# Attention and gated layer on one core: the inner layer's columns dealt in pairs

## The chip, the cores and the metric

The kernel runs on one core of one Trainium2 chip. The metric is the device time of one execution in microseconds. Three runs of the kernel before gave a median of 287.04 us (286.77 to 288.16).

## The reference

Inputs are float32: q, k and v of 8 batches, 8 heads, 576 positions and 64 channels; `w_in` (512 x 2048), `w_out` (2048 x 512) and `beta` (2048).

```python
q_s = softmax(q, over the channels);  k_s = softmax(k, over the positions)
kv  = einsum('bhsd,bhse->bhde', k_s, v)
att = einsum('bhsd,bhde->bhse', q_s, kv)
x   = att.transpose(0, 2, 1, 3).reshape(4608, 512)
h   = x @ w_in
g   = h * (1 / (1 + exp(-beta * h)))
out = g @ w_out
```

The 2048 columns of `w_in` are the rows of `w_out` and the entries of `beta`: the inner layer. Any order of them gives the same sum, so long as all three use the same.

## The kernel before

The five engines take their instructions from one list of named steps, `ORDER` at the top of the file, written out by hand; each engine takes its own steps in that order, and SP issues nearly all the loads and stores. A layer under the kernel adds the semaphore waits: where an instruction touches what an instruction of another engine wrote or still reads, it waits for that one.

*Attention.* Per batch b, `ld q`, `ld k`, `ld v` bring in the inputs; DVE takes maxima (`qmax`, `kmax`), POOL subtracts them (`qsub`, `ksub`), ACT takes exponentials (`qexp`, `kexp`), DVE sums and inverts (`qsum`, `qrcp`), POOL normalises (`qnorm`). PE multiplies k by v (`kv`, line 638), transposes q (`qtr`, line 464; later batches by DMA) and forms x transposed (`x`, line 688), which ACT and DVE cast into `xT` (`xev`).

*Inner layer.* The 4608 rows of x make 9 chunks of 512. A chunk has 16 units u of 128 inner columns. Step `h n` (n = 16 x chunk + u, function `st1`, line 889) is four matmuls, one for each contraction tile kt of 128: the weights are a 128 x 128 block of `w_in_b`, the moving side 512 columns of `xT`, the result a bank of PSUM. `th n` (ACT, line 907) takes the tanh with the scale in `beta_c[:, u]`, `g n` (DVE, line 924) makes the gated value, and `o n` (`st2`, line 959) multiplies it by `w_out_b[:, u, :]` into four accumulators. In the first chunk the first four units are cut into halves of 256 columns (`h 0 0 0`: unit 0, half 0, contraction tiles 0 and 2; `h 0 0 1`: tiles 1 and 3), and the order is h 0, 1, 2, 3, 6, 4, 5, 7, then 8, 10, 9, 11 with the transposes of batch 1 between.

*Weights.* They come in eight blocks `w0` to `w7`, in turn `w_in` and `w_out`: w0, w2, w4, w6 are 512 columns each of `w_in`, w1, w3, w5, w7 are 512 rows each of `w_out`. A block comes in two halves (`ld w2 0`, `ld w2 1`), each 512 KB, into one of four float32 stages `wst`; a half of a `w_in` block is two of the four contraction tiles. `cast w2 0` and so on turn a half into bfloat16, on POOL or ACT as `ORDER` says. Block w0 is cast in two parts, so that unit 0 is ready early: columns 0 to 127 (`cast w0 0 0`, `cast w0 1 0`) and 128 to 511 (`cast w0 0 1` on POOL, `cast w0 1 1` on ACT). `w_in_b` holds 2048 columns for each contraction tile, in their own order.

*Beta.* One DMA brings `beta` as 16 rows of 128; PE transposes it (line 345) and ACT copies it into `beta_c`, one column for each unit.

Step names of POOL around the change, in its order: `cast w0 0 1`, `qsub 1 0`, `qnorm 0 2`, `cast w2 0`, `cast w2 1`, `qsub 1 1`, `cast w1 0`, `cast w1 1`, `cast w4 0`, `qnorm 1 0`, `qnorm 1 1`, `cast w3 0`, `cast w6 0`.

Of the kernel before, what the change touches and what calls it, by code (L numbers as in the profile page):

```python
# [8 lines left out]
BF16 = mybir.dt.bfloat16  # L9
F32 = mybir.dt.float32  # L10
ALU = mybir.AluOpType
ACTF = mybir.ActivationFunctionType
# [105 lines left out]
def kernel(  # L118
# [11 lines left out]
    P = 128  # L130
    B, H, S, D = q.shape
    DM, FF = w_in.shape
# [4 lines left out]
    KT = DM // P  # L137
    NJ = FF // P
# [13 lines left out]
    def op(name, fn, eng=None):  # L152
        assert name not in ops, name
        ops[name] = (fn, eng)
# [4 lines left out]
    def sbt(name, shape, dt):  # L159
        return sb.tile(shape, dt, name=name)  # L160

    ident_f = sbt("ident_f", [P, P], F32)
# [2 lines left out]
    minus = sbt("minus", [P, P], F32)  # L165
    warm = sbt("warm", [P, P], BF16)
    first = sbt("first", [P, 1], F32)
    beta_rows = sbt("beta_rows", [NJ, P], F32)
    beta_c = sbt("beta_c", [P, NJ], F32)
    w_in_b = sbt("w_in_b", [P, KT, FF], BF16)  # L170
    w_out_b = sbt("w_out_b", [P, NJ, DM], BF16)
    wst = [sbt(f"wst{i}", [P, 4, 512], F32) for i in range(4)]
    qf = [sbt(f"qf{i}", [P, KT, NI, D], F32) for i in range(2)]
# [21 lines left out]
    th = [sbt(f"th{i}", [P, 512], BF16) for i in range(3)]  # L195
# [5 lines left out]
    place = {}  # L201
# [4 lines left out]
    def take(*who):  # L206
        assert sum(last in done for last, _ in turns) >= len(who), who
        for w in who:
            n = next(n for n, (last, _) in enumerate(turns) if last in done)
            i = turns.pop(n)[1]  # L210
            place[w] = ring[i][:]
            turns.append((w, i))

    def made(what, *parts):
        done.update((what, p) for p in parts)

    def uses(what, *parts):
        for p in parts:
            assert (what, p) in done, (what, p)
# [7 lines left out]
    dve, act, pool, pe, sp = nc.vector, nc.scalar, nc.gpsimd, nc.tensor, nc.sync  # L227
    ENGINES = {"act": act, "dve": dve, "pool": pool}

    def cast(eng, dst, src):  # L230
        if eng is act:
            act.copy(dst, src)  # L232
        else:
            eng.tensor_copy(dst, src)  # L234
# [57 lines left out]
    for b in range(B):  # L292
        n = 2 if b else 1
# [4 lines left out]

    W = [(w, blk) for blk in range(4) for w in ("i", "o")]
    w_in_v = w_in.rearrange("(kt p) f -> p kt f", p=P)
    w_out_v = w_out.rearrange("(j p) f -> p j f", p=P)

    def load_w(n, half):
        which, blk = W[n]
        if n > 3:
            which, blk = W[n - 4]
            if which == "i":
                uses("i", *[(4 * blk + u, half) for u in range(4)])  # L310
            else:
                uses("o", 2 * blk + half)
            which, blk = W[n]
        dst = wst[n % 4][:, 2 * half : 2 * half + 2, :]
        if which == "i":
            sp.dma_start(dst, w_in_v[:, 2 * half : 2 * half + 2, 512 * blk : 512 * blk + 512])
        else:
            sp.dma_start(dst, w_out_v[:, 4 * blk + 2 * half : 4 * blk + 2 * half + 2, :])

    def cast_w(n, half, eng, c0=0, c1=512):  # L320
        which, blk = W[n]
        s = wst[n % 4][:, 2 * half : 2 * half + 2, c0:c1]
        if which == "i":
            made("i", *[(4 * blk + c // P, half) for c in range(c0, c1, P)])
            cast(eng, w_in_b[:, 2 * half : 2 * half + 2, 512 * blk + c0 : 512 * blk + c1], s)
        else:
            made("o", 2 * blk + half)
            cast(eng, w_out_b[:, 4 * blk + 2 * half : 4 * blk + 2 * half + 2, :], s)

    for n in range(8):  # L330
        for half in range(2):
            op(f"ld w{n} {half}", lambda n=n, half=half: load_w(n, half))
            if n == 0:
                for c, (c0, c1) in enumerate(((0, P), (P, 512))):
                    op(
                        f"cast w{n} {half} {c}",
                        lambda e, n=n, half=half, c0=c0, c1=c1: cast_w(n, half, e, c0, c1),
                        "pool",
                    )
            else:  # L340
                op(f"cast w{n} {half}", lambda e, n=n, half=half: cast_w(n, half, e), "pool")

    def beta_tr():
        take("beta")
        pe.transpose(place["beta"][:, 0:NJ], beta_rows[:], ident_f[0:NJ, 0:NJ])

    def beta_ev():
        done.add("beta")
        act.copy(beta_c[:], place["beta"][:, 0:NJ])

    op("ld beta", lambda: sp.dma_start(beta_rows[:], beta.rearrange("(j p) -> j p", p=P)))
    op("beta tr", beta_tr)
    op("beta ev", beta_ev)

# [427 lines left out]
    for h in range(3):  # L782
        i0, i1 = 4 * h, min(4 * h + 4, NI)
        for J in range(2):
            p = dict(j=2 * J, n=2, i0=i0, i1=i1)
# [57 lines left out]
    def chunk_x(c):  # L843
        if c == TAILS:
            return xTt
        return xT[(c if c < TAILS else c - 1) % 2]

    def halves(h):
        return (0, 1) if h is None else (h,)

    def cols(h):
        return slice(0, 512) if h is None else slice(256 * h, 256 * h + 256)
# [3 lines left out]
    def bank(n, h):  # L856
        key = ("h", n) if h is None else ("hp", n // 2, h)
        if key not in place:
            take(key)
        if h is None:  # L860
            return place[key]
        return place[key][:, 256 * (n % 2) : 256 * (n % 2) + 256]

    def turn(n, h):
        return n if h is None else 2 * (n // 2) + h

    def st1(n, ks=(0, 1, 2, 3), h=None):
        c, u = divmod(n, NJ)
        x = chunk_x(c)
        for kt in ks:  # L870
            uses("i", (u, kt // 2))
            if c == TAILS:
                uses("xTt", *[(b, kt % 2) for b in range(B)])
            else:
                uses("xT", *[(c - (c > TAILS), kt, a) for a in halves(h)])
        if h is not None and n % 2 and ks[0] == 0:
            uses("st1", (n - 1, h))
        if ks[0]:
            uses("begun", (n, h))
        made("begun", (n, h))  # L880
        w = bank(n, h)
        if c == 0 and h is None:
            w = w.rearrange("p (h c) -> p h c", h=2)
        for kt in ks:
            r = x[:, kt, cols(h)]
            if c == 0:
                r = x_first[:, kt % 2, kt // 2]
                r = r if h is None else r[:, h]
            pe.matmul(  # L889
                w,  # L890
                w_in_b[:, kt, u * P : (u + 1) * P],
                r,
                start=(kt == 0),
                stop=(kt == KT - 1),
            )
        if KT - 1 in ks:
            made("st1", *[(n, a) for a in halves(h)])

    def tanh(n, h=None):
        u = n % NJ  # L900
        mates = [n] if h is None else [2 * (n // 2), 2 * (n // 2) + 1]
        uses("st1", *[(m, a) for m in mates for a in halves(h)])
        if turn(n, h) >= 3:
            uses("gated", turn(n, h) - 3)
        made("tanh", *[(n, a) for a in halves(h)])
        c = cols(None if h is None else n % 2)
        act.activation(th[turn(n, h) % 3][:, c], bank(n, h), ACTF.Tanh, scale=beta_c[:, u : u + 1])  # L907

    def gate(n, h=None):
        mates = [n] if h is None else [n, n + 1]  # L910
# [88 lines left out]
    for n in range(NU):  # L999
        if n < LEAD:  # L1000
            for h in range(2):
                for x in range(2):
                    op(f"h {n} {h} {x}", lambda n=n, h=h, x=x: st1(n, (x, x + 2), h))
                op(f"th {n} {h}", lambda n=n, h=h: tanh(n, h))
                if n % 2 == 0:
                    op(f"g {n} {h}", lambda n=n, h=h: gate(n, h))
                op(f"o {n} {h}", lambda n=n, h=h: st2(n, h))
            continue
        if n in (16, 17):
            op(f"h {n} 0", lambda n=n: st1(n, (0, 1)))  # L1010
            op(f"h {n} 1", lambda n=n: st1(n, (2, 3)))
        else:
            op(f"h {n}", lambda n=n: st1(n))
        op(f"th {n}", lambda n=n: tanh(n))
        op(f"g {n}", lambda n=n: gate(n))
        if n >= NU - LAST:
            for t in range(3):
                op(f"o {n} {t}", lambda n=n, t=t: st2(n, ts=[t]))
            for x in range(2):
                op(f"o {n} 3 {x}", lambda n=n, x=x: st2(n, ts=[3], xs=[x]))  # L1020
        else:
            op(f"o {n}", lambda n=n: st2(n))
# [12 lines left out]
    with tc.manual_schedule():  # L1035
        for name, _, e in plan:
            fn, eng = ops[name]
            eng = e or eng
# [31 lines left out]
```

## Time and profile before

| | |
|---|---|
| median of three runs | 287.04 us |
| the profiled execution's time | 287.31 us |
| its span, first to last instruction | 285.5 us |
| PE busy in the span | 275.8 us (97%) |
| weight loads busy | 129.9 us (45%) |
| DVE, ACT, POOL busy | 194.9, 174.2, 131.2 us |
| `w_out` loads, 8 of 512 KB, from issue to landing | 11.2 us |
| `w_in` loads, 8 of 512 KB, from issue to landing | 7.9 us |

All times come from one execution. PE is TensorE's matmuls, PEld its weight loads, which overlap the matmuls; DVE is VectorE, ACT ScalarE, POOL GpSimd, SP the engine that issues DMAs. Rows of a group give line, engine, operation, output and input tiles with shapes and count, then busy time and mean duration in ns, then the idle time of the engine just before and what ended it. Rows of the timeline give start and duration in us, and rows of the chain of waits start, duration and what the chain ran through.

### The profile page before, as it was taken

Reading aid. Unit: us, or ns where it says so; the run is one execution under the profiler, and the core shown is the slowest. Engines: PE = TensorE matmul, PEld = TensorE weight load, DVE = VectorE, ACT = ScalarE, POOL = GpSimd, SP = SyncE. Lnnn points to the kernel's source line nnn. Section 1 sums busy time; section 2 is a strip of 40 time slices with the busy share of each in tenths; the row PEclk is TensorE's granted clock in tenths of the full one; section 3 lists DMA queues with packets and bytes.
Section 4 is the critical chain, followed back from the end, with each engine's and each line's share of the span. In section 5 each row is a group of like instructions: output and inputs, shape, how many; then the busy total and the mean of one; then the engine's idle time right before and its main releaser. Section 6 shows DMA issues by size and latency. Waiting matters only on the chain.

```text
span 285.5 us, 5163 instructions
## 1 busy us (share of the span) xinstructions
PE 275.8 (97%) x1947; PEld 129.9 (45%) x1977; DVE 194.9 (68%) x394; ACT 174.2 (61%) x291; POOL 131.2 (46%) x93
## 2 busy tenths in 40 slices
PE   7799999999999999999999999999999999999994
PEld 2356544444444544444444544444444444444442
DVE  2998957999899898997667858555754263435421
ACT  2498885887488577837586566564671274345422
POOL 6899996869379948083960650090020000000000
PEclk9999999999999999999999999999999999999999
DMA  7999999990991994991434927000054001005104
GB/s 229 390 391 385 384 389 391 390 336 7 276 371 43 316 275 181 295 329 41 152 119 113 189 62 193 0 3 2 0 141 164 0 0 39 0 0 187 73 0 147
DMA packets 37048, 50.01 MB, mean 175 GB/s; under 512 B 15760, under 2 KB 16160, under 8 KB 37024
## 3 DMA queue, kind: packets, MB, share of 16 engines
q1 hardware_dynamic: 36880, 49.63, 53.4%
q8 instruction: 15, 0.25, 0.3%
q10 hardware_dynamic: 144, 0.07, 0.1%
q14 instruction: 9, 0.07, 0.1%
HBM read 36.71 MB, written 9.44 MB: 162 GB/s over the span
## 4 chain that ended last, share of the span: by engine, by line
PE 91%; DMA 4%; ACT 1%; SPq 1%; issue 1%; DVE 0%
PE hT L889 43%; PE acc L959 42%; DMA kf<-in_k_dram 2%; DMA wst<-in_moe_w_in_dram 2%; PE hT L638 2%; PE hT L688 1%; SPq L275 1%; PE hT L951 1%; PE acc L951 1%; ACT w_in_b L232 0%; PE hT L464 0%; PE hT L734 0%; ACT qT L232 0%; ACT ek L612 0%; ACT ek L605 0%
## 5 line engine op out<-in xcount | busy, mean ns | idle before, releaser
L907 ACT ACTIVATE th<-hT,beta_c 128x512 bf16<-128x512 f32 (+1 forms) x148 | 96.6, 677 | 66.9 <-PE hT L889 48.5
L924 DVE SCALAR_TENSOR_TENSOR g<-th,hT 128x512 bf16<-128x512 bf16 x144 | 94.6, 680 | 58.5 <-ACT th L907 55.5
L959 PE MATMUL acc<-w_out_b,g 128*128 128x512 bf16 x543 | 130.7, 379 | 1.4 <-issue 0.8
L889 PE MATMUL hT<-xT,w_in_b 128*128 128x512 bf16 (+1 forms) x517 | 117.7, 372 | 0.7 <-issue 0.2
L889 PEld LDWEIGHTS <-w_in_b 128*128 128x128 bf16 x592 | 57.6, 98 | 64.8 <-ACT w_in_b L232 0.2
L959 PEld LDWEIGHTS <-g 128*128 128x128 bf16 x560 | 53.7, 98 | 64.5 <-issue 2.9
L560 POOL TENSOR_TENSOR kf<-kf,kmb 128x1152 f32<-128x1152 f32 (+1 forms) x15 | 38.0, 2543 | 23.6 <-DVE kmb L550 17.6
L441 POOL TENSOR_TENSOR qn<-eqe,qz 128x1152 bf16<-128x1152 bf16 (+2 forms) x20 | 34.5, 1739 | 28.0 <-DVE qz L433 18.1
L393 POOL TENSOR_TENSOR qf<-qf,qm 128x1152 f32<-128x1152 f32 (+2 forms) x20 | 34.4, 1733 | 18.4 <-issue 11.9
L378 DVE TENSOR_REDUCE qm<-qf 128x9 f32<-128x576 f32 (+2 forms) x34 | 23.3, 704 | 6.2 <-DMA qf<-in_q_dram 6.2
L422 ACT ACTIVATE eqe<-qf 128x576 bf16<-128x576 f32 (+2 forms) x34 | 21.5, 657 | 9.5 <-POOL qf L393 9.5
L232 ACT CAST xT<-hT 128x512 bf16<-128x512 f32 x19 | 12.6, 740 | 21.1 <-PE hT L688 21.1
L428 DVE TENSOR_REDUCE qs<-eqe 128x9 f32<-128x585 bf16 (+2 forms) x34 | 24.0, 713 | 0.5 <-ACT eqe L422 0.4
L490 DVE TRANSPOSE_TENSOR_REDUCE km<-kf 128x18 f32<-128x576 f32 x32 | 23.6, 754 | 0.0
L612 ACT ACTIVATE ek<-kf 128x576 bf16<-128x576 f32 x30 | 19.5, 683 | 0.9 <-DMA vf<-in_v_dram 0.9
L234 POOL CAST va<-vf 128x1152 bf16<-128x1152 f32 (+1 forms) x11 | 12.0, 1105 | 6.9 <-DMA vf<-in_v_dram 6.9
L889 PE MATMUL hT<-xTt,w_in_b 128*128 128x512 bf16 x63 | 14.9, 379 | 0.1
L234 DVE CAST xT<-hT 128x512 bf16<-128x512 f32 x9 | 6.3, 728 | 7.0 <-PE hT L688 7.0
L232 ACT COPY osb<-acc 128x512 f32<-128x512 f32 x14 | 7.8, 594 | 3.0 <-PE acc L959 3.0
L367 PE MATMUL hT<-g,warm 128*128 128x512 bf16 x21 | 7.0, 482 | 1.6 <-POOL g L240 1.5
L234 DVE COPY osb<-acc 128x512 f32<-128x512 f32 (+1 forms) x6 | 3.8, 632 | 4.9 <-PE acc L951 3.8
L638 PEld LDWEIGHTS <-ek 64*64 64x64 bf16 x576 | 5.7, 106 | 2.2 <-issue 1.3
(74 smaller groups left out, 121.7 us busy)
## 6 DMA issues: line engine op xcount, KB each, us to landing
qf<-in_q_dram SPq DMA_DIRECT2D x14, 576.0 KB, 6.9
kf<-in_k_dram SPq DMA_DIRECT2D x14, 576.0 KB, 7.7
vf<-in_v_dram SPq DMA_DIRECT2D x14, 576.0 KB, 8.4
out_dram<-osb SPq DMA_DIRECT2D x19, 256.0 KB, 2.6
wst<-in_moe_w_in_dram SPq DMA_DIRECT2D x8, 512.0 KB, 7.9
wst<-in_moe_w_out_dram SPq DMA_DIRECT2D x8, 512.0 KB, 11.2
out_dram<-wst SPq DMA_DIRECT2D x16, 256.0 KB, 3.7
qf<-in_q_dram SPq DMA_DIRECT2D x4, 288.0 KB, 4.1
```

Of the source, the lines that this page charges most:

```text
L234: eng.tensor_copy(dst, src)
L378: dve.tensor_reduce(qm[:, j : j + n, i0:i1], qf[b % 2][:, j : j + n, i0:i1], axis=AX.X, op=ALU.max,)
L393: eng.tensor_tensor(x, x, m, ALU.subtract)
L422: act.activation(eq[:, i0:i1, j : j + n, :].rearrange("p i j d -> p j i d"), x, ACTF.Exp)
L428: dve.tensor_reduce(qs[:, i0:i1, j : j + n].unsqueeze(3), x, axis=AX.X, op=ALU.add)
L441: eng.tensor_tensor(qn[b % 2][:, i0:i1, j : j + n, :], eq[:, i0:i1, j : j + n, :], z, ALU.mult)
L490: dve.tensor_reduce(km[:, j : j + n].rearrange("p j i e -> p (j i e)"), kf[b % 2][:, j : j + n].rearrange("p j i (e c) -> p (j i e) c", c=32),
L560: eng.tensor_tensor(x, x, m, ALU.subtract)
L889: pe.matmul(w, w_in_b[:, kt, u * P : (u + 1) * P], r, start=(kt == 0), stop=(kt == KT - 1),)
L907: act.activation(th[turn(n, h) % 3][:, c], bank(n, h), ACTF.Tanh, scale=beta_c[:, u : u + 1])
L924: dve.scalar_tensor_tensor(out=out, in0=of, scalar=1.0, in1=src, op0=ALU.add, op1=ALU.mult)
L959: pe.matmul(acc[t][:], g[n % NG][:, t * P : (t + 1) * P], w_out_b[:, u, :], start=(u == 0), stop=(u == NJ - 1),)
```

## The change

Inner columns are dealt in pairs of units. A pair m covers 256 columns of `w_in`; its even columns make unit 2m, its odd ones unit 2m + 1. A partition of `w_out`'s block then holds two rows that follow each other in memory, 4 KB, where it held two runs of 2 KB.

For `w_in` nothing changes on the side of the load. The cast writes a pair's 256 columns into a block of 320 (64 are never used), and a matmul's weights are read with a step of two. Casts of whole blocks write three free dimensions: two contraction tiles, two pairs, 256 columns. Block w0 is cast in parts of 256 and 256 columns. `beta` is read as 8 rows of 256, transposed in two pieces with a step of two, and the tanh finds its scale in the column of the new order.

```diff
-    beta_rows = sbt("beta_rows", [NJ, P], F32)
+    beta_rows = sbt("beta_rows", [NJ // 2, 2 * P], F32)
...
-    w_in_b = sbt("w_in_b", [P, KT, FF], BF16)
+    w_in_b = sbt("w_in_b", [P, KT, NJ // 2, 2 * P + 64], BF16)
...
-    w_out_v = w_out.rearrange("(j p) f -> p j f", p=P)
+    w_out_v = w_out.rearrange("(m p r) f -> p m r f", p=P, r=2)
...
-            sp.dma_start(dst, w_out_v[:, 4 * blk + 2 * half : 4 * blk + 2 * half + 2, :])
+            sp.dma_start(dst, w_out_v[:, 2 * blk + half])
...
-            cast(eng, w_in_b[:, 2 * half : 2 * half + 2, 512 * blk + c0 : 512 * blk + c1], s)
+            m0, m1 = 2 * blk + c0 // (2 * P), 2 * blk + c1 // (2 * P)
+            s = s.rearrange("p k (m c) -> p k m c", c=2 * P)
+            cast(eng, w_in_b[:, 2 * half : 2 * half + 2, m0:m1, 0 : 2 * P], s)
...
-                for c, (c0, c1) in enumerate(((0, P), (P, 512))):
+                for c, (c0, c1) in enumerate(((0, 2 * P), (2 * P, 512))):
...
-        pe.transpose(place["beta"][:, 0:NJ], beta_rows[:], ident_f[0:NJ, 0:NJ])
+        for r in range(2):
+            n = NJ // 2
+            pe.transpose(place["beta"][:, n * r : n * r + n], beta_rows[:, r : 2 * P : 2], ident_f[0:n, 0:n])
...
-    op("ld beta", lambda: sp.dma_start(beta_rows[:], beta.rearrange("(j p) -> j p", p=P)))
+    op("ld beta", lambda: sp.dma_start(beta_rows[:], beta.rearrange("(m q) -> m q", q=2 * P)))
...
-                w_in_b[:, kt, u * P : (u + 1) * P],
+                w_in_b[:, kt, u // 2, u % 2 : 2 * P : 2],
...
+        v = NJ // 2 * (u % 2) + u // 2
...
-        act.activation(th[turn(n, h) % 3][:, c], bank(n, h), ACTF.Tanh, scale=beta_c[:, u : u + 1])
+        act.activation(th[turn(n, h) % 3][:, c], bank(n, h), ACTF.Tanh, scale=beta_c[:, v : v + 1])
```

The list of steps is the same.

## The prediction

> **What bounds the kernel now.** I read the windows first, then the chain of waits.
>
> ```profile
> 20.30:62.00 41.70, 41.38 (x292) 20.91 (x296) 34.91 (x73) 33.86 (x58) 34.14 (x26) 1.00 1.05 388
> 62.00:281.90 219.90, 218.03 (x1510) 101.30 (x1533) 146.10 (x287) 128.93 (x211) 81.07 (x39) 1.00 0.41 120
> ...
> 20.29 0.38 PE hT L367
> 20.67 7.01 PE hT L889 x48
> 27.68 0.22 PE acc L959
> ...
> 31.24 0.86 PE hT L889 x4
> 32.11 0.45 PE hT L464 x8
> 32.55 1.73 PE hT L889 x8
> ...
> 37.32 3.46 PE hT L889 x16
> ```
>
> Columns of a window: stretch, length, then busy time of PE, weight loads, DVE, ACT and POOL, granted clock, DMA share, GB/s. From 20.3 us on PE is idle for 0.32 us up to 62 us and for 1.87 us up to 281.9 us, and the chain runs through PE almost without a break. Sixteen matmuls take 3.46 us, 216 ns each. So a PE stall after 20.3 us moves the end one for one, and a transfer or cast that comes earlier moves nothing. The DMA is full until 62 us (388 GB/s), but PE hides it.
>
> **Where the change bites: two waits in the order of work.** The casts of whole `w_in` blocks now write three free dimensions (two contraction tiles, two pairs, 256 columns) where two served before. I resolved the semaphores of both built programs to the instructions that raise them. PE's order is the same apart from one more small transpose, but these waits are new:
>
> ```
> PE   h 0 0 1, contraction tile 1 (reads w_in_b from element 2560)  waits for POOL cast w2 0
> PE   h 0 0 1, contraction tile 3 (reads from 7680)                 waits for POOL cast w2 1
> PE   h 10,    contraction tile 1 (reads from 4160)                 waits for POOL cast w6 0
> POOL cast w4 0 waits for PE h 7;  POOL cast w6 0 waits for PE h 8
> ```
>
> None carries data. Cast w2 0 starts at element 640 and ends at 640 + 2560 + 320 + 255 = 3775; h 0 0 1 reads 2560 to 2814, between the written rows. It looks as if a pattern of this many dimensions is compared by its whole span; the two-dimensional casts of before gave no such wait. Before, w2 was first waited for by h 6 and w6 by h 14. Whatever the cause, the waits stand in the program, and PE takes its instructions in order, so all the matmuls behind wait too, and ACT's tanh and DVE's gate behind them.
>
> **First stall.** POOL, in order of time:
>
> ```profile
> 18.20 0.82 POOL L234 CAST w_in_b<-wst 128x768 bf16<-128x768 f32 x1
> 18.98 2.12 POOL L393 TENSOR_TENSOR qf<-qf,qm 128x1152 f32<-128x1152 f32 x1
> 21.05 0.76 POOL L441 TENSOR_TENSOR qn<-eqe,qz 128x128 bf16<-128x128 bf16 x2
> 21.75 2.02 POOL L234 CAST w_in_b<-wst 128x1024 bf16<-128x1024 f32 x2
> 24.01 2.12 POOL L393 TENSOR_TENSOR qf<-qf,qm 128x1152 f32<-128x1152 f32 x1 [0.23 <-DVE qm L378]
> 26.07 2.02 POOL L234 CAST w_out_b<-wst 128x1024 bf16<-128x1024 f32 x2
> 28.03 1.04 POOL L234 CAST w_in_b<-wst 128x1024 bf16<-128x1024 f32 x1
> 29.66 4.31 POOL L441 TENSOR_TENSOR qn<-eqe,qz 128x1152 bf16<-128x1152 bf16 x2 [0.58 <-ACT th L907]
> 33.91 1.03 POOL L234 CAST w_out_b<-wst 128x1024 bf16<-128x1024 f32 x1
> 34.88 1.04 POOL L234 CAST w_in_b<-wst 128x1024 bf16<-128x1024 f32 x1
> ```
>
> Casts w2 0 and w2 1 are the pair at 21.75; the second ends at 23.77. POOL is busy without a gap from 18.20 to there, so they wait for POOL's turn, not for their load. The cast at 18.20 shrinks from 768 to 512 columns. By these rows:
>
> ```profile
> L234 POOL CAST w_in_b<-wst 128x1024 bf16<-128x1024 f32 x4 | 4.1, 1039 | 0.0
> L234 POOL CAST w_in_b<-wst 128x768 bf16<-128x768 f32 x1 | 0.8, 824 | 0.0
> L232 ACT CAST w_in_b<-wst 128x768 bf16<-128x768 f32 x1 | 0.8, 832 | 0.0
> L232 ACT CAST w_in_b<-wst 128x256 bf16<-128x256 f32 x2 | 0.9, 432 | 0.0
> ```
>
> 256 columns cost POOL 1039 - 824 = 215 ns, so cast w2 1 ends at 23.77 - 0.21 = 23.56. With about 0.15 us for semaphore and weight load (an estimate: POOL's start at 24.01 comes 0.09 us after the end of DVE's row at 23.18 below, and a weight load stands some 0.1 us long) the fourth matmul of the stage, which stood at 20.67 + 3 x 0.11 = 21.0, starts at 23.7. First stall: 2.7 us (2.5 to 2.95, the upper end without the shorter cast).
>
> **Second stall.** What follows on POOL hangs on PE again:
>
> ```profile
> 22.57 0.69 DVE L924 SCALAR_TENSOR_TENSOR g<-th,hT 128x512 bf16<-128x512 bf16 x1 [0.75 <-ACT th L907]
> 23.18 0.74 DVE L378 TENSOR_REDUCE qm<-qf 128x9 f32<-128x576 f32 x1
> 25.99 0.69 ACT L907 ACTIVATE th<-hT,beta_c 128x512 bf16<-128x512 f32 x1 [0.24 <-PE hT L889]
> 27.72 0.68 ACT L422 ACTIVATE eqe<-qf 128x576 bf16<-128x576 f32 x1
> 29.25 0.26 DVE L433 RECIPROCAL qz<-qs 128x18 f32<-128x18 f32 x1
> ```
>
> POOL's subtraction at 24.01 waits for the maximum at 23.18, which stands on DVE behind the first gate, which waits for tanh. The normalisation at 29.66 waits for the reciprocal at 29.25, whose exponential stands on ACT behind tanh of h 4, which waits for PE. So both move by 2.7 us with PE. From 29.66 POOL works without a gap to the end of cast w6 0 at 34.88 + 1.04 = 35.92. The matmul of h 10 that now waits for it stood at 32.55 + 0.22 = 32.77. Both are 2.7 us later, so the gap stays: 35.92 + 0.15 - 32.77 = 3.3 us. If POOL's chain moved by less than PE, the stall would shrink; the only play is POOL's 0.58 us of idleness before 29.66 and ACT's slack, so 2.7 to 3.3; I take 3.2. POOL's own two new waits don't bind: h 7 ends by 27.68 + 2.7 = 30.4, when POOL is just through the casts of `w_out` (28.1 + 2.7 = 30.8), and h 8 by 32.11 + 2.7 = 34.8 against 37.6 for cast w6 0.
>
> After it no new wait is left. POOL and the loads are then ahead of PE, so nothing else turns late; the later idle time of PE is scattered in pieces of about 0.1 us and gives back 0 to 0.3 us.
>
> **The rest of the change.** ACT's three part casts become 512 columns each: 832 + 2 x 432 = 1696 ns become 3 x 632 (halfway between the rows) = 1896, 0.2 us more. The second transpose for beta costs 0 to 0.23 us of PE. Both come ahead of 21 us and are hidden by the first stall; without it they would cost 0.1 to 0.4 us. The `w_out` loads in 4 KB runs could shorten the DMA's work, at most by what is visible as PE's idleness before 62 us, 0.32 us; I take nothing, since PE hides them. Weight loads with a step of two have no row. Their neighbours:
>
> ```profile
> L889 PEld LDWEIGHTS <-w_in_b 128*128 128x128 bf16 x592 | 57.6, 98 | 64.8 <-ACT w_in_b L232 0.2 <-issue 0.2
> L638 PEld LDWEIGHTS <-ek 64*64 64x64 bf16 x576 | 5.7, 106 | 2.2 <-issue 1.3 <-ACT ek L612 0.5 <-DVE qs L428 0.4
> L580 PEld LDWEIGHTS acc<-kf,ident_f 128*128 128x128 f32 x4 | 0.7, 188 | 1.3 <-issue 1.2
> 20.57 2.50 PEld L889 LDWEIGHTS <-w_in_b 128*128 128x128 bf16 x23 [0.18 <-issue]
> ```
>
> The lower bound is 98 ns as now, the upper one the float32 row, 188 ns, whose columns also lie four bytes apart. Both fit under the 216 ns of a 512-column matmul. Only the first 32 matmuls are half as wide (23 loads in 2.50 us, 109 ns each): at 188 ns they cost 32 x (188 - 109) = 2.5 us. I take 98, because the 0.1 us of loads is pipelined; the upper end goes into the range.
>
> **Sum.** Against the profiled execution's 287.31 us (span 285.5 and 1.8 around it): + 2.7 + 3.2 - 0.2 = 293.0 us. That execution lies 0.27 above the median of 287.04, so 292.8 for a median; I say 292.9.
>
> **Rivals.**
>
> *The clock drops in the stalls.* PE stands still for 1.7 and 0.9 us with one matmul between, and then for 3.2 us, longer than any gap in its record of before. At the start of the span matmuls run at half pace:
>
> ```profile
> 1.45 5.45 PE L367 MATMUL hT<-g,warm 128*128 128x512 bf16 x16 [1.45 <-POOL g L240]
> 4.39 0.15 PEld L367 LDWEIGHTS <-warm 128*128 128x128 bf16 x1 [0.28 <-issue]
> 4.82 0.15 PEld L367 LDWEIGHTS <-warm 128*128 128x128 bf16 x1 [0.28 <-issue]
> ```
>
> 430 ns between weight loads against 216, from 1.45 to about 5.2. If a stall brings that back for as long, it costs 3.75 / 2 = 1.9 us: 294.8 for one, 296.7 for both. The Trainium skill (TensorE: Matmul & The Clock Gate, Part 1) says that an idle window of about 3.4 us halves the clock until a busy window has passed; the second stall lies just under that, so by the rule the case is open. Against it: the stall is short of that start-up phase.
>
> *The step of two shows* as well, in the half-wide matmuls, up to 2.5 us: 295.4.
>
> *Only the first stall bites.* If POOL's normalisations and casts run early enough, h 10 waits for little: 287.1 + 2.7 = 289.8. It needs POOL's chain to come loose from PE; the two rows with waits above speak against it.
>
> *No stall.* The two casts at 21.75 are through before h 0 0 1 asks, at 20.9, and cast w6 0 before 32.8: then only part casts and the beta transpose remain, 287.2, not slower. The point is whether POOL gets to those casts 2.8 us earlier; its rows show 2.9 us of other work ahead of them, in order, which makes this unlikely.
>
> **How the numbers follow.** Forecast 0.56 (own range 292.0 to 293.7), clock 0.20, step of two 0.08, first stall alone 0.10, no stall 0.06. The range takes in the forecast, one drop of the clock and a step of two: 291.0 to 295.5; outside lie the first stall alone, no stall and both drops. 0.5% (1.4 us) is about what a measurement can tell from no change. Only "no stall" is not slower by that: same 0.04, faster 0.02 (a gain that no row shows), slower 0.94.
>
> **What would show it.** Right: in the profile after, PE idle near 21 to 23.6 us and near 35.5 to 38.7 us, both put down to POOL's casts of `w_in_b`; from there the same chain, some 6 us late; 216 ns a matmul. The strided load's row gives its duration, and spacing of 430 ns after a stall would mean the clock. Wrong: PE without those gaps, or a loss spread evenly over all matmuls of line 889, which would be the price of the strided weights.

## The result and the profile after

The changed kernel takes 296.2 us (median of four executions, 294.29 to 296.58) against 287.06 us for the kernel before: ratio 1.0298, interval 1.027 to 1.0326. The forecast was 292.9 with a range of 291.0 to 295.5: the direction holds, the time lies above the range. The profiled execution is the quickest of the four, 294.29 us with a span of 292.5.

The stretches of the span that answer to the prediction's first rows, in the changed kernel (start and end, length, busy us of PE, weight loads, DVE, ACT, POOL, then granted clock, DMA share, GB/s):

```profile
20.30:62.00 41.70, 36.26 (x260) 18.11 (x261) 27.70 (x55) 27.86 (x47) 29.82 (x23) 0.96 0.90 336
62.00:285.00 223.00, 223.00 (x1543) 102.15 (x1542) 152.17 (x302) 133.09 (x218) 84.39 (x41) 1.00 0.42 126
```

Everything is lost between 20.3 and 62 us. PE was idle there for 0.32 us before and is for 41.70 - 36.26 = 5.44 us now, and its mean clock fell from 1.00 to 0.96. Behind 62 us nothing is lost. PE's waits, summed by what ended them (us in total, times, longest):

```profile
PE hT L894 <- POOL w_in_b L234: 5.6, 3, 3.2
PE hT L372 <- POOL g L240: 1.5, 1, 1.5
```

PE's timeline of the changed kernel shows where the three are (line 894 was 889, 965 was 959):

```profile
19.76 0.38 PE L894 MATMUL hT<-xT,w_in_b 128*128 128x256 bf16 x2
21.83 0.28 PE L894 MATMUL hT<-xT,w_in_b 128*128 128x256 bf16 x1 [1.69 <-POOL w_in_b L234]
22.82 6.79 PE L894 MATMUL hT<-xT,w_in_b 128*128 128x256 bf16 x45 [0.70 <-POOL w_in_b L234]
29.45 1.89 PE L965 MATMUL acc<-w_out_b,g 128*128 128x512 bf16 x8
...
34.32 0.38 PE L894 MATMUL hT<-xT,w_in_b 128*128 128x512 bf16 x1
37.91 3.11 PE L894 MATMUL hT<-xT,w_in_b 128*128 128x512 bf16 x7 [3.21 <-POOL w_in_b L234]
```

The stage that starts here at 19.76 started at 20.57 before. In the other kernels below it starts between 19.16 and 20.63 us, at 19.76 and 20.58 in the two whose time is that of the kernel before, and at 20.05 in a second profile of the changed kernel, so this is taken for spread between executions and not for the change. POOL's casts, in order of time in the same execution:

```profile
20.74 2.02 POOL L234 CAST w_in_b<-wst 128x1024 bf16<-128x1024 f32 x2
25.94 2.12 POOL L398 TENSOR_TENSOR qf<-qf,qm 128x1152 f32<-128x1152 f32 x1 [3.18 <-DVE qm L383]
...
31.59 4.31 POOL L446 TENSOR_TENSOR qn<-eqe,qz 128x1152 bf16<-128x1152 bf16 x2 [0.59 <-ACT th L913]
35.84 1.04 POOL L234 CAST w_out_b<-wst 128x1024 bf16<-128x1024 f32 x1
36.81 1.04 POOL L234 CAST w_in_b<-wst 128x1024 bf16<-128x1024 f32 x1
```

PE goes on at 21.83 and 22.82, just behind the first and the second of the casts at 20.74, and at 37.91, 0.06 us behind the end of the one at 36.81. That is the forecast chain: POOL's subtraction waits 3.18 us for the maximum that hangs on PE, and POOL's idleness before 31.59 is 0.59 us as it was 0.58.

The last of those PE rows holds what the forecast did not have: seven 512-column matmuls in 3.11 us, where eight took 1.73 in the chain of before. PE's weight loads behind the second stall:

```profile
38.26 0.15 PEld L894 LDWEIGHTS <-w_in_b 128*128 128x128 bf16 x1 [0.24 <-issue]
38.69 0.15 PEld L894 LDWEIGHTS <-w_in_b 128*128 128x128 bf16 x1 [0.28 <-issue]
39.11 0.15 PEld L894 LDWEIGHTS <-w_in_b 128*128 128x128 bf16 x1 [0.27 <-issue]
39.54 0.15 PEld L894 LDWEIGHTS <-w_in_b 128*128 128x128 bf16 x1 [0.28 <-issue]
```

They are 430 ns apart: half pace, the sign that the prediction named for the clock. The stretch that holds them says the same in its third number from the right, the granted clock, which is half of what it was (such a spell at half clock is called a drop from here on):

```profile
37.90:41.30 3.40, 3.39 (x12) 1.51 (x13) 1.22 (x3) 0.92 (x2) 2.75 (x2) 0.52 1.04 396
```

In this execution the first stall has no such sequel (45 matmuls in 6.79 us). The mean granted clock of a span tells how many drops it has: half pace for 3.4 us (the length of a drop, worked out in the last section) takes 1.7 / 292.5 = 0.6% off. The kernel before, without a drop, shows 0.997 to 1.000. The profiled execution shows 0.994, one drop; the three others show 0.988, 0.988 and 0.987, two.

The group that was to show a price of the strided weights:

```profile
L894 PEld LDWEIGHTS <-w_in_b 128*128 128x128 bf16 x592 | 57.8, 98 | 71.7 <-POOL w_in_b L234 6.4 <-issue 1.3
```

and the page's row of DMA issues (KB each, us to landing) for the longer runs:

```profile
wst<-in_moe_w_out_dram SPq DMA_DIRECT2D x8, 512.0 KB, 8.3
```

A weight load with a step of two takes 98 ns, as without it. The `w_out` loads land in 8.3 us where they took 11.2; the third experiment says how much of that is the 4 KB.

### The profile page after: what moved, and what is told of

Read it like the earlier page. It is cut to its first block, busy times and chain, and to the rows that moved or that the text cites. A ratio compares the mean times of both kernels' runs of the same rounds, so it can differ in the third digit from the quotient of the medians.

```text
span 292.5 us, 5196 instructions
## 1 busy us (share of the span) xinstructions
PE 280.9 (96%) x1978; PEld 130.8 (45%) x1978; DVE 195.1 (67%) x394; ACT 174.9 (60%) x291; POOL 131.0 (45%) x93
## 4 chain that ended last, share of the span: by engine, by line
PE 87%; DMA 4%; DVE 3%; POOL 1%; ACT 1%; SPq 1%; issue 1%; DVEq 0%; POOLq 0%
PE acc L965 41%; PE hT L894 40%; DMA kf<-in_k_dram 2%; PE hT L643 2%; DMA qf<-in_q_dram 2%; PE hT L693 1%; DVE km L495 1%; SPq L275 1%; POOL qn L446 1%; DVE qs L433 1%; PE hT L957 1%; PE acc L957 1%; PE acc L598 1%; DVE qm L383 1%; ACT th L913 0%
## 5 line engine op out<-in xcount | busy, mean ns | idle before, releaser
L965 PE MATMUL acc<-w_out_b,g 128*128 128x512 bf16 x560 | 133.0, 379 | 0.0
L894 PE MATMUL hT<-xT,w_in_b 128*128 128x512 bf16 (+1 forms) x528 | 120.5, 376 | 5.6 <-POOL w_in_b L234 5.6
L372 PE MATMUL hT<-g,warm 128*128 128x512 bf16 x22 | 8.3, 536 | 1.5 <-POOL g L240 1.5
L372 PEld LDWEIGHTS <-warm 128*128 128x128 bf16 x30 | 3.6, 124 | 7.2 <-issue 5.5
```

The source lines that it names most:

```text
L894: pe.matmul(w, w_in_b[:, kt, u // 2, u % 2 : 2 * P : 2], r, start=(kt == 0), stop=(kt == KT - 1),)
L965: pe.matmul(acc[t][:], g[n % NG][:, t * P : (t + 1) * P], w_out_b[:, u, :], start=(u == 0), stop=(u == NJ - 1),)
```

## The experiments

The theory after this reading: three waits for casts that carry no data stall PE (some 6 us), and the clock drops behind the stalls (some 3 us). To be told apart: what in the change makes the waits (the padding, the number of dimensions of the casts, the step of two), whether the clock's part is real and how large, and whether anything else is gained or lost beneath them.

**Without the 64 columns of padding.** The cast of a block then writes 512 columns that lie side by side, as before the change.

```diff
-    w_in_b = sbt("w_in_b", [P, KT, NJ // 2, 2 * P + 64], BF16)
+    w_in_b = sbt("w_in_b", [P, KT, NJ // 2, 2 * P], BF16)
```

> The changed kernel without the 64 padding columns, so that a cast of a whole w_in block writes two free dimensions (2 x 512) again; weights are still read with a step of two. The waits theory in its first form (a pattern of four dimensions is compared by its whole span) would expect the waits gone and 287 us. But the built program still has them: h 0 0 1 waits for casts w2 0 and w2 1, h 10 for cast w6 0. So the waits theory in its second form (the read with a step of two is what is compared by its span) expects the same time as with the padding, 294 to 296.5 us, and the same two gaps on PE, about 2.5 and 3.2 us. A theory in which the padded layout itself costs time expects clearly less than with it.

296.24 us (296.09 to 297.12) against 287.22, ratio 1.0305 (1.0276 to 1.0334). The waits are all there; from PE's timeline of this kernel:

```profile
19.16 0.38 PE L894 MATMUL hT<-xT,w_in_b 128*128 128x256 bf16 x2
21.32 0.28 PE L894 MATMUL hT<-xT,w_in_b 128*128 128x256 bf16 x1 [1.77 <-POOL w_in_b L234]
23.42 8.09 PE L894 MATMUL hT<-xT,w_in_b 128*128 128x256 bf16 x45 [1.82 <-POOL w_in_b L234]
```

So neither the padding nor a third dimension made by it is the cause. The last gap is 1.82 instead of 0.70 us because this execution started the stage earlier and POOL's second cast, for once, waited for its load (POOL's timeline):

```profile
22.32 1.04 POOL L234 CAST w_in_b<-wst 128x1024 bf16<-128x1024 f32 x1 [1.06 <-DMA wst<-in_moe_w_in_dram]
```

The 45 matmuls take 8.09 instead of 6.79 us: here the first stall too is followed by a drop, as these stretches of the same kernel show (clock third from the right):

```profile
21.00:22.00 1.00, 0.28 (x1) 0.10 (x1) 0.00 (x0) 0.00 (x0) 0.26 (x1) 1.00 1.01 391
22.00:23.30 1.30, 0.00 (x0) 0.00 (x0) 0.00 (x0) 0.00 (x0) 0.98 (x1) 0.77 1.02 395
23.30:24.30 1.00, 0.88 (x5) 0.64 (x6) 0.00 (x0) 0.00 (x0) 0.06 (x1) 0.50 1.06 391
24.30:25.30 1.00, 1.00 (x6) 0.70 (x5) 0.00 (x0) 0.54 (x2) 0.00 (x0) 0.50 1.05 388
...
26.30:28.00 1.70, 1.70 (x18) 1.52 (x16) 1.37 (x3) 1.40 (x4) 0.93 (x1) 1.00 1.06 393
```

**Padding and casts of three free dimensions, but weights read side by side.** The kernel before with the padded tile, the changed kernel's casts and its parts of 256 and 256 columns; the columns are not dealt, so `w_out` and `beta` stay as they were.

```diff
-                w_in_b[:, kt, u // 2, u % 2 : 2 * P : 2],
+                w_in_b[:, kt, u // 2, (u % 2) * P : (u % 2) * P + P],
```

> The kernel before with the padded layout, the four-dimensional casts and block w0 cast in two parts of 256, but a unit's 128 columns side by side as before (no step of two, no pairs in w_out and beta). Its program has none of the new waits. The waits theory expects 287 us, within 0.3%; a theory in which padding or four-dimensional casts cost time expects a part of the 9 us.

287.28 us (286.64 to 287.91), ratio 1.0003 (0.9986 to 1.002). Line 234's casts of `w_in_b` are gone from PE's waits in this kernel:

```profile
PE hT L369 <- POOL g L240: 1.5, 1, 1.5
PE acc L466 <- POOL qn L443: 1.1, 1, 1.1
PE hT L369 <- ACT eqe L424: 0.8, 1, 0.8
```

The same casts with the same dimensions cause no stall as long as the weights are read side by side. What the prediction took for the reason falls.

**The changed kernel with each cast of a whole block in two, one for each contraction tile.** All else stays: dealt columns, 4 KB runs, step of two, padding.

```diff
-            cast(eng, w_in_b[:, 2 * half : 2 * half + 2, m0:m1, 0 : 2 * P], s)
+            if n:
+                for k in range(2):
+                    cast(eng, w_in_b[:, 2 * half + k, m0:m1, 0 : 2 * P], s[:, k])
+            else:
+                cast(eng, w_in_b[:, 2 * half : 2 * half + 2, m0:m1, 0 : 2 * P], s)
```

> The changed kernel with each cast of a whole w_in block issued as two, one for each contraction tile (2 x 256 columns each), so that none of the three waits stands in the program; padding, step of two, pairs, 4 KB runs stay. The waits theory expects the whole loss gone: 286.5 to 288 us, no gap on PE near 21 and 35 us. A theory in which strided weights cost time expects most of the loss to stay, with weight loads longer than 98 ns or matmuls of line 889's kind further apart than 216 ns.

287.51 us (286.67 to 287.7, ten executions), ratio 0.9997 (0.9981 to 1.0013): the whole loss is gone. From PE's timeline of this kernel:

```profile
20.58 7.27 PE L898 MATMUL hT<-xT,w_in_b 128*128 128x256 bf16 x48
27.68 1.89 PE L969 MATMUL acc<-w_out_b,g 128*128 128x512 bf16 x8
...
32.56 1.89 PE L898 MATMUL hT<-xT,w_in_b 128*128 128x512 bf16 x8
...
35.60 1.89 PE L969 MATMUL acc<-w_out_b,g 128*128 128x512 bf16 x8
```

its group of weight loads:

```profile
L898 PEld LDWEIGHTS <-w_in_b 128*128 128x128 bf16 x592 | 57.6, 98 | 64.9 <-ACT w_in_b L232 0.2 <-issue 0.2
```

and its DMA issues:

```profile
wst<-in_moe_w_out_dram SPq DMA_DIRECT2D x8, 512.0 KB, 10.5
```

No gap is left, and everything else that the change brings is, taken together, worth nothing measurable in either direction: the weights with a step of two, the part casts, the second transpose, the longer runs. The run does not part them from each other. The `w_out` loads, still in 4 KB runs, land in 10.5 us against 11.0 in the kernel of the second experiment with its runs of 2 KB. So most of the way from 11.2 down to the 8.3 of the changed kernel goes with its stalls and not with the longer runs.

Together with the second experiment this gives the cause of the waits: a read with a step of two that meets a write across two contraction tiles. Tile 1 of h 0 0 1 reads elements 2560, 2562 and so on up to 2814; cast w2 0 writes 640 to 1215 in tile 0 and 3200 to 3775 in tile 1. They share nothing, but 2560 to 2814 lies within 640 to 3775. A write of one tile alone no longer spans it, and a read side by side is told apart from it all the same. It fits that the waits are placed by the span of the strided read against the span of the write; how the layer under the kernel decides was not looked at.

**One stall at a time.** The same edit for block w2 alone (`if n == 2:`) takes the first stall away:

> The changed kernel with only block w2's casts split by contraction tile: h 0 0 1 waits for nothing new, h 10 still waits for cast w6 0. Waits and clock: one gap of 3.2 us on PE near 35 us, and as it is longer than the 1.7 and 1.8 us gaps that were not always or just followed by half pace, the clock drops each time: 287.2 + 3.3 + 1.8 = 292.3 us (291.8 to 292.8). If the gap alone cost time: 290.5. If the step of two cost something elsewhere, more than 292.8.

and for w4 and w6 alone (`if n > 2:`) the second:

> The changed kernel with only blocks w4 and w6 split: h 0 0 1 still waits for casts w2 0 and w2 1, h 10 for nothing new. The two stalls add, so with the kernel above it should make up the changed kernel's 9.1 us: 9.1 - 5.1 = 4 us, 291.2 us where the clock drops after the first stall (as in the run with a granted clock of 0.988) and 289.5 where it doesn't (0.994). Near 287 would mean that the first stall costs nothing of its own.

291.91 us (290.91 to 292.62) with the second stall alone, ratio 1.0154 (1.0131 to 1.0176), and 291.45 (291.39 to 291.75) with the first alone, 1.0145 (1.0125 to 1.0164); the kernel before stood at 287.17. The parts, 4.7 and 4.3, add up to 9.0, which is the whole loss (8.9 on the same chip, below). PE's timeline with the second stall alone:

```profile
19.97 7.28 PE L898 MATMUL hT<-xT,w_in_b 128*128 128x256 bf16 x48
...
35.56 3.09 PE L898 MATMUL hT<-xT,w_in_b 128*128 128x512 bf16 x7 [3.21 <-POOL w_in_b L234]
```

and with the first alone:

```profile
20.63 0.38 PE L898 MATMUL hT<-xT,w_in_b 128*128 128x256 bf16 x2
22.70 0.32 PE L898 MATMUL hT<-xT,w_in_b 128*128 128x256 bf16 x1 [1.69 <-POOL w_in_b L234]
23.68 8.02 PE L898 MATMUL hT<-xT,w_in_b 128*128 128x256 bf16 x45 [0.66 <-POOL w_in_b L234]
...
36.41 1.89 PE L898 MATMUL hT<-xT,w_in_b 128*128 128x512 bf16 x8
```

The second stall is 3.21 us long without the first as well: it is not the first one's echo, but POOL's place in the order against h 10. In both profiles the stall is followed by half pace (7 matmuls in 3.09 us, 45 in 8.02). Half pace behind the second stall was expected each time, but of the five executions with that stall alone one shows a mean clock of 1.000.

**The stalls kept, PE kept busy in them.** First with the kernel's own `fill` steps, matmuls of zeros whose results are not used: 9 ahead of h 0 0 1 and 15 ahead of h 10.

```diff
-    FILLS = [(14, None)] + [(2, (h, J)) for h in range(2) for J in range(2)] + 8 * [(1, None)]
+    FILLS = [(14, None)] + [(2, (h, J)) for h in range(2) for J in range(2)] + 8 * [(1, None)] + 3 * [(3, None)] + 3 * [(5, None)]
```

> The changed kernel with matmuls of zeros put where PE stands still: 9 ahead of h 0 0 1 and 15 ahead of h 10 (216 ns each, 1.9 and 3.2 us); their results are not used. The waits stay. If the clock drops because PE is idle, it stays up now: no 430 ns matmuls after the gaps, 292.3 to 293 us, and a narrow spread of times. If the clock has no part in it, the time stays 294 to 296.5 us or grows.

294.07 us (293.56 to 294.32), ratio 1.0217 (1.0186 to 1.0248), 1 us above what was expected. The clock stayed up (0.999), but the fills took banks of the ring, and so PE got a wait that the changed kernel does not have:

```profile
25.91 5.36 PE L894 MATMUL hT<-xT,w_in_b 128*128 128x256 bf16 x32 [0.84 <-DVE g L930]
```

So this run says that the clock counts, but not how much. It was done again with matmuls that write into the bank that is next free, without taking a turn of the ring, 8 and 14 of them, results unused:

```diff
+    def warm_up(n):
+        i = next(i for last, i in turns if last in done)
+        for _ in range(n):
+            pe.matmul(ring[i][:], warm[:], g[NG - 1], start=True, stop=True)
```

> The changed kernel with its three waits and matmuls of zeros in the gaps as before (8 ahead of h 0 0 1, 14 ahead of h 10), but written into the bank that is next free, without taking a turn in the ring of banks, so that they bring no wait for a gate. Waits without the clock: 287.2 + 2.5 + 3.2 = 292.9 us (292.3 to 293.3), granted clock 0.998 or more, no pace of 430 ns after 20 us. If it lies at 294 again, the matmuls of zeros themselves or the stalls cost more than the gaps show.

293.28 us (292.77 to 293.62), ratio 1.0205 (1.0184 to 1.0226). PE's timeline:

```profile
19.91 0.38 PE L901 MATMUL hT<-xT,w_in_b 128*128 128x256 bf16 x2
20.12 1.89 PE L377 MATMUL hT<-g,warm 128*128 128x512 bf16 x8
...
22.95 6.79 PE L901 MATMUL hT<-xT,w_in_b 128*128 128x256 bf16 x45 [0.70 <-POOL w_in_b L234]
29.59 1.89 PE L972 MATMUL acc<-w_out_b,g 128*128 128x512 bf16 x8
...
38.05 1.69 PE L901 MATMUL hT<-xT,w_in_b 128*128 128x512 bf16 x7 [0.19 <-POOL w_in_b L234]
...
40.88 1.89 PE L972 MATMUL acc<-w_out_b,g 128*128 128x512 bf16 x8
```

The useful matmuls go on where they do in the changed kernel: 22.95 and 38.05 are 3.04 and 18.14 us behind the start of the stage, 22.82 and 37.91 there 3.06 and 18.15. But seven take 1.69 us and not 3.11. The waits alone cost 293.28 - 287.17 = 6.1 us.

**The changed kernel again**, beside these on the same chip:

> The changed kernel as it is, on the same chip as the three others: 296.2 us with granted clock 0.988 (both stalls followed by half pace) in most executions, 294.3 with 0.994 (only the second) in some; nothing between. A spread without two groups would speak against the clock as what parts them.

296.05 us (294.53 to 297.22, six executions), ratio 1.0309 (1.028 to 1.0337). The clock's part is 296.05 - 293.28 = 2.8 us. Of the ten executions of the changed kernel in all, seven show a mean clock of 0.987 or 0.988, 295.81 to 297.22 us, and three 0.994, 294.29 to 294.77.

No kernel here beats the one before; with the casts split the change is free, and that is all.

## Why the prediction was right or wrong

*PE as the bound, one for one: right.* The kernel with split casts has no stall and no loss; each stall moved the end by itself, and where the clock stayed up the two, 2.6 and 3.4 us as read below, cost 6.1.

*Three new waits, their places and holders: right. Their reason: wrong.* "A pattern of this many dimensions is compared by its whole span" falls with the second experiment; it takes the step of two in the read and the write over two tiles together. The forecast did not hang on it, since the waits were read from the program.

*First stall, 2.7 us (2.5 to 2.95): right.* From the first matmul of the stage to the first of the next it takes 29.59 - 19.91 = 9.68 us in the kernel that kept the clock up, against 27.68 - 20.58 = 7.10 with split casts: 2.6 us.

*Second stall, 3.2 us (2.7 to 3.3): right within 0.2, just above its range.* From there to the next `w_out` stage 40.88 - 29.59 = 11.29 against 35.60 - 27.68 = 7.92: 3.4 us. POOL moved with PE as said, and POOL's own two new waits don't show on its rows. The 0.2 us given back later did not come. The forecast, which holds no drop of the clock, was 292.9 (its terms on the median give 287.04 + 5.7 = 292.7); the kernel with the warming matmuls, where no drop comes, shows 293.28.

*Strided weights, part casts, transpose, 4 KB runs, all at nothing: right together,* by the split casts' ratio of 0.9997. Its interval, 0.9981 to 1.0013, does not rule out the 0.1 to 0.4 us that the prediction gave the part casts and the transpose where no stall hides them.

*The clock: the step that failed.* It had a chance of 0.20, and the case of both drops was left outside the range. The argument was that the stall "is short of that start-up phase". That phase, 1.45 to about 5.2 us, tells how long PE worked until the pace doubled; how long it must stand until the pace halves is another matter, and in the profile of before PE's longest gap behind the start is 1.1 us. Nor does any run show that the two slow phases are one thing: the trace's granted clock reads 1.00 in the start-up phase (before, 2.5 to 5 us) and 0.50 behind the stalls. The runs showed that a stall of 3.2 us can be enough (half pace in all four profiles that have the second stall without matmuls put into it, though not in one of the executions with it alone), and that 1.7 and 0.7 us with one matmul between are enough in most executions. The Trainium skill (TensorE: Matmul & The Clock Gate, Part 1) states the window of some 3.4 us as one that runs freely and does not start anew with a kernel; the prediction used its length as if it were the length of a gap. The edges of the drops in the profiles agree with such a window (last section).

Price of a drop: taken as 1.9 us each. Behind the second stall, 42.42 - 37.91 = 4.51 us pass in the changed kernel between h 10's second matmul and the next `w_out` stage, 40.88 - 38.05 = 2.83 with warming: 1.7 us. (42.42 is the start of this row of the changed kernel's PE timeline.)

```profile
42.42 1.89 PE L965 MATMUL acc<-w_out_b,g 128*128 128x512 bf16 x8
```

Behind the first it is 8.09 - 6.79 = 1.3 us, because the drop begins while PE still stands. The sum as it ought to have been: 287.1 + 2.6 + 3.4 + 1.3 + 1.7 = 296.1, against 296.2 measured. The rival's own price for both drops, 296.7, was 0.5 us off; the fault was its chance, and a range that left both drops out.

## What to carry to other kernels

Before a layout is changed so that an operand is read with a step, list the semaphore waits of the built program: a strided read and a write over several tiles that share no byte can still be ordered, and one instruction more (the cast in two) undoes it. In this kernel a new stall of some 2 to 3 us on the matmul engine cost the stall itself and, in most executions, 1.3 to 1.7 us more at half clock; a forecast for a like stall should have that drop within its range. A gain off the path (the 4 KB loads under a PE that is busy throughout) was worth nothing here, and what it cost elsewhere was the whole result.

## What the runs showed of the hardware that was not expected

The drops stand on a grid. Four stretches of 0.1 us in the kernel without padding hold the edges of its two drops:

```profile
22.60:22.70 0.10, 0.00 (x0) 0.00 (x0) 0.00 (x0) 0.00 (x0) 0.10 (x1) 0.98 1.01 389
26.10:26.20 0.10, 0.10 (x3) 0.06 (x2) 0.10 (x1) 0.00 (x0) 0.00 (x0) 0.95 0.98 366
39.70:39.80 0.10, 0.00 (x0) 0.00 (x0) 0.09 (x1) 0.00 (x0) 0.06 (x1) 0.81 0.61 110
43.10:43.20 0.10, 0.10 (x4) 0.10 (x3) 0.00 (x0) 0.10 (x1) 0.10 (x1) 0.62 1.36 346
```

A clock of 0.98 in the first says that it fell from 1 to 0.5 at 22.60 + 0.096 = 22.70; the others give 26.11, 39.76 and 43.18. The distances are 3.41, 13.65 (four times 3.41) and 3.42 us: they fit a clock that is decided once in 3.41 us, and both drops last one such window. The stalls do not set these times. Here PE stops at 19.16 + 0.38 = 19.54 and the clock falls 3.16 us later; with the first stall alone PE stops at 20.63 + 0.38 = 21.01, and by the edge in this stretch of that kernel the clock falls at 22.82, 1.81 us later:

```profile
22.80:22.90 0.10, 0.10 (x1) 0.00 (x0) 0.00 (x0) 0.00 (x0) 0.10 (x1) 0.61 1.09 389
```

In the kernel without padding the window from 19.28 to 22.70 holds less than 0.6 us of PE's work, and the clock drops at its end. In the changed kernel's profile the drop is at 38.0; counted back from there the first stall lies in the window from 20.9 to 24.4, more than half of which is work, and no drop follows. So the first stall can be followed by a drop, which costs 1.3 us, or not. That its place in the window decides this is a reading of these edges, which no run tested. How idle a window must be stays open: the six windows that ended in a drop held 0.2 to 1.62 us of PE's work, the last of these with the first stall alone, and the two that held most of the first stall without a drop, in the two profiles of the changed kernel, held 1.66 and 1.82. The execution with the second stall alone and a mean clock of 1.000 took 291.45 us, no less than the quickest of its kernel with a drop (290.91, clock 0.994); it was not profiled.
